# Backward of a gated linear-attention and feed-forward block on one core: grouped row-tile ends, a row vector spread through DRAM, other first loads

## The chip, the cores and the metric

The kernel runs on one core of a Trainium2 chip. The time is the device time of one execution in microseconds (us); lower is better. The kernel before took 638.77 us, the median of nine runs that lay between 637.89 and 639.11. The core has a matrix engine (TensorE, PE in the profile, with its weight loads as PEld), a vector engine (DVE), a scalar engine (ACT), a general engine (GpSimd, POOL) and a queue engine (SyncE, SP) that here issues transfers only. ACT issues transfers too. The engines run side by side, each in its own order, and wait for one another through semaphores.

## What is computed

The reference is a forward pass and its gradients. With x of 2048 tokens by 640, 32 heads of 20, and 1728 hidden columns:

```python
g = sigmoid((x * gate_w).sum(-1, keepdims=True))
q, k, v = heads of x @ wqkv
phi = lambda t: where(t > 0, t + 1, exp(t)) + 1e-6
kv = einsum("bhsd,bhse->bhde", phi(k), v)
z  = einsum("bhsd->bhd", phi(k))
o  = (phi(q) @ kv) / (phi(q) . z + 1e-6)
a  = o @ wo
b  = maximum(x @ w1, 0) @ w2
out = g * a + (1 - g) * b
```

The outputs are `out` and the gradients by x, wqkv, wo, w1, w2 and gate_w, all in bf16.

## The kernel before

The 2048 tokens are NT = 16 tiles of 128, in NG = 4 groups of G = 4. The 640 columns are KD = 5 blocks of 128. The 1728 hidden columns are KF = 14 blocks, of which the last has FT = 64 columns: its matmuls use half of the array's rows.

All long-lived data lie in one large buffer, the arena. A planner gives each named piece an offset and a life by nominal times (`ar.add(name, bytes, t0, t1)`, lines 113 to 189); pieces whose lives don't overlap share room. A change of one entry can therefore move other pieces. Small tiles come from pools: `tb` (8 buffers), `f32` (3), and PSUM tiles from `pp` (line 306), four buffers of two banks each. Code is written in program order, and the compiler's scheduler then orders each engine's instructions by priority and readiness; dependencies become waits. Only the opening stretch has its PE order fixed by hand (line 478).

The stages, in order, with their lines:

- k stage (399 to 511). First loads of x tiles 0 to 4 and the five blocks of wk, from SP and ACT. A few matmuls on a zeroed tile (`warm_up`) run until data are there. Tiles 0 to 4 of x are transposed on PE (`xt`), the rest by transposing transfers. Then k = x wk for each tile (`k_part`), with phi by `phi_chain`: exp on ACT, then two DVE operations (396, 397).
- Y stage (626 to 635). Y = phi(k)^T x, one 128-row block at a time. An extra column of ones in x gives z as a column of each block; it is copied to `zc_t`. To have z as a row on all partitions (`zb`), a diagonal matrix `zd` is made of each block of z, and a matmul of ones by `zd` (`zp`, 637 to 639) gives the row in PSUM; ACT copies it to `zb`. `q_den` (526) multiplies phi(q) by `zb` on POOL, and `q_post` (530) reduces the product on DVE.
- q, feed-forward forward and output (612 to 689). `h_half` makes half of a tile's hidden row, `out_chunk` the output. Here too `tail_pair` (579) ends two neighbouring tiles' sums together.
- dw2 and the gradient by q's factors (730 to 775), then X (801 to 808).
- The feed-forward backward (811 to 957), described below.
- dk (`dk_chunk`, 881) between halves of dw1 (`dw1_half`, 899), then dwk, dwq and dx (983 on).

In the feed-forward backward, `fb_a(i, half)` computes half of tile i's hidden gradient (PSUM tile `gp`), scales it on ACT, masks it on DVE, and after the second half starts the transposing transfer into a slot of the ring `hTb`. `fb_b(i)` multiplies the transposed tile by w1^T into a PSUM tile `dp`: thirteen blocks of two matmuls (512 and 128 columns, `mm_cols`, line 339), and the fourteenth block through `tail_pair`. That one runs two matmuls side by side, each on 64 rows: one ends tile i, the other starts tile i+1, for which a second `dp` is opened:

```python
nc.tensor.matmul(psA[:, b, 0:e - a], lhsT=lA[0:FT], rhs=rhs[0:FT, a:e], start=False, stop=last)
nc.tensor.matmul(psB[:, b, 0:e - a], lhsT=lB[FT:P], rhs=rhs[FT:P, a:e], start=True, stop=False)
```

So a tail pair comes once for every two tiles. ACT copies each finished `dp` out, and stores two tiles together to DRAM. The loop runs `fb_b` four tiles behind `fb_a`. Between them stand small products (`small_0` to `small_3`, PSUM tiles dwo, bd, qqp, dwv) and many loads. In iteration 14 of the loop the four groups of x^T for dk (`xSg`) and the first two loads of phi(k) are asked for.

Of the kernel before, what the change touches and what calls it, by code (L numbers as in the profile page):

```python
# [8 lines left out]
ALU = mybir.AluOpType  # L9
AX = mybir.AxisListType  # L10
FP32 = mybir.dt.float32
BF16 = mybir.dt.bfloat16
PSUM = bass.MemoryType.PSUM

P = 128
# [66 lines left out]
def kernel(  # L82
# [34 lines left out]
    def ring(name, elems, count, t0, t1):  # L117
        ar.add(name, elems * count * B2, t0, t1)
        rings[name] = [elems, count, 0]
# [13 lines left out]
    ar.add("w1", KD * F * B2, 8, T_H)  # L133
    ar.add("w2", KF * D * B2, 12, T_DW2 + 10)
    ar.add("pk", NT * D * B2, 0, T_FF)
    ar.add("zd", D * B2, 0, T_FF - 5)
    ar.add("YT0", KD * D * B2, T_Y, T_FF + 5)
    ar.add("dzs", D * B2, T_X, T_FB + 50)
    ar.add("warm", 512 * B2, 0, 10)
# [26 lines left out]
    ar.add("dKVT", KD * D * B2, T_FB + 40, T_FB + 65)  # L166
    ar.add("Q", KD * D * B2, T_FB + 58, T_DWK - 10)
    ar.add("N", KD * D * B2, T_DWK, T_END)
    ring("hTb", KF * P, 5, T_FB, T_DW1 + 5)
    ring("wst", D, 4, T_FB + 88, T_FB + 112)  # L170
    ar.add("dwoT", KD * D * B2, T_FB + 15, T_FB + 52)
    ar.add("dwo", KD * D * B2, T_FB + 45, T_FB + 80)
    ring("dxst", 2 * D, 2, T_FB + 5, T_DW1 + 5)
    ar.add("xN2", NT * D * B2, T_DW1 - 25, T_DX + 5)
    for g in range(NG):
        ar.add(f"xS{g}", G * P * KD * B2, T_DW1 - 25, T_DWK - 10)
        ar.add(f"dk{g}", G * D * B2, T_DW1 + 5 + 15 * g, T_DX)
        ar.add(f"dkT{g}", G * D * B2, T_DW1 + 5 + 15 * g, T_END)
    ring("pkr", 2 * D, 3, T_DW1 - 20, T_DWK)
# [15 lines left out]
    def aview(name, n_elems, **dims):  # L195
        o = ar.off(name) // 2
        v = arena[:, o:o + n_elems]
        if dims:
            (k, n), = dims.items()
            v = v.rearrange(f"p ({k} z) -> p {k} z", **{k: n})  # L200
        return v
# [7 lines left out]
    def mat(name):  # L209
        return aview(name, KD * D, k=KD)  # L210
# [15 lines left out]
    xSg = [aview(f"xS{g}", G * D, k=KD) for g in range(NG)]  # L226
    doTg = [aview(f"doT{g}", G * D, k=KD) for g in range(NG)]
    hsg = [aview(f"hs{g}", G * FPAD, i=G) for g in range(NG)]
    zd, YT0_s = aview("zd", D), mat("YT0")
    dzs = aview("dzs", D)  # L230
    wk_s, wq_s, wv_s, wo_s = aview("wk", KD * DQX, k=KD), mat("wq"), mat("wv"), mat("wo")
    w1_s = aview("w1", KD * F, k=KD)
# [30 lines left out]

    dram = ctx.enter_context(tc.tile_pool(name="dram", bufs=1, space=bass.MemoryType.DRAM))
    pk_d = dram.tile([S, D], BF16, name="pk_d")
    pqg_d = dram.tile([S, D], BF16, name="pqg_d")
    KVT_d = dram.tile([D, D], BF16, name="KVT_d")
    e_d = dram.tile([S, D], BF16, name="e_d")
# [14 lines left out]
                            pattern=[[-1, P]], channel_multiplier=1)  # L283
    gwb = cpool.tile([P, D], BF16, name="gwb")
    ones_sq = cpool.tile([P, P], BF16, name="ones_sq")
    zc_t = cpool.tile([P, KD], FP32, name="zc_t")
    MDw = cpool.tile([P, KD, BWID], BF16, name="MDw")
    zb = cpool.tile([P, D], BF16, name="zb")
    dzb = cpool.tile([P, D], BF16, name="dzb")
# [16 lines left out]
    def pp(name="pp"):  # L306
        return psp.tile([P, 2, 512], FP32, tag="PP", bufs=4, name=_nm(name))
# [4 lines left out]
    def csl(i):  # L312
        return slice(i * P, (i + 1) * P)

    def flat(ps_tile):
        return ps_tile.rearrange("p b c -> p (b c)")
# [16 lines left out]
    def load_N(dst, src):  # L333
        return nc.sync.dma_start(dst, src.rearrange("(i p) d -> p i d", p=P))
# [15 lines left out]
    def halves(ap):  # L350
        return ap.rearrange("p (b c) -> p b c", b=2)
# [47 lines left out]

    warm = aview("warm", 512)  # L400
    nc.vector.memset(warm, 0.0)
    def x_load(a, b):
        return load_N(xN[:, a:b, 0:D], x2[a * P:b * P, :])

    def wk_load(eng, k):
        eng.dma_start(wk_s[:, k, 0:D], A_wqkv[k * P:(k + 1) * P, D:2 * D])

    nc.scalar.dma_start(gst[:], gate_w.rearrange("(k p) -> k p", p=P))
    x_load(0, 1)
    wk_load(nc.scalar, 0)  # L410
    x_load(1, 2)
    wk_load(nc.scalar, 1)
    x_load(2, 3)
    wk_load(nc.scalar, 2)
    wk_load(nc.sync, 3)
    wk_load(nc.sync, 4)
    for i in range(3, NPE):
        x_load(i, i + 1)
# [40 lines left out]
    def warm_up(n, cols=512):  # L459
        for _ in range(n):  # L460
            nc.tensor.matmul(wp_[:, 0, 0:cols], lhsT=warm[:, 0:P], rhs=warm[:, 0:cols], start=True, stop=True)
# [16 lines left out]
    with tc.manual_schedule(engines={mybir.EngineType.PE}):  # L478
        warm_up(4)
        warm_up(1, 256)  # L480
        xt(0)
        tp = psp.tile([P, KD, P], BF16, tag="PP", bufs=4, name="gwtp")
        nc.tensor.transpose(tp[:, 0, 0:KD], gst[:], ident[0:KD, 0:KD])
        nc.vector.tensor_copy(wk_s[:, :, D:D + 1], tp[:, 0, 0:KD].unsqueeze(2))
        warm_up(3)
        k_part(0, [0])
        xt(1)
        xt(2)
        k_part(1, [0])
        k_part(0, [1])  # L490
        k_part(1, [1])
        k_part(2, [0, 1])
        k_part(0, [2])
        after(xT_ld[0], k_part(1, [2]), wait=True)
        k_part(2, [2])
        k_part(0, [4, 3])
        xt(3)
        k_part(1, [4, 3])
        xt(4)
        k_part(2, [4, 3])  # L500
        k_part(3, range(KD))
        k_part(4, range(KD))
# [123 lines left out]
    for m in range(KD):  # L626
        yp = pp("yp")
        for i in range(NT):
            mm_cols(yp, pkN[:, i, csl(m)], lambda a, e: xN[:, i, a:e], i == 0, i == NT - 1, spl=DSP1)
        yt = nc.scalar.copy(YT0_s[:, m, :], flat(yp)[:, 0:D])  # L630
        if m == 0:
            masks(yt)
        nc.vector.tensor_copy(zc_t[:, m:m + 1], flat(yp)[:, D:D + 1])
        nc.vector.tensor_scalar(zd[:, csl(m)], ident[:], zc_t[:, m:m + 1], None, ALU.mult)
        Y_ld = load_T(Y_s[:, :, csl(m)], YT0_s[:, m, :])
    h_half(0, 0)
    zp = pp("zp")
    mm_cols(zp, ones_sq[:], lambda a, e: zd[:, a:e], True, True)
    nc.scalar.copy(zb[:], flat(zp)[:, 0:D])
    q_den(0)  # L640
    h_half(0, 1)
    h_half(1, 0)
# [186 lines left out]
            load_T(dhTs[i], hs(i))  # L829

    def fb_b(i):
        pr, ii = i // 2, i % 2
        dT = dhTs.pop(i)
        if ii == 0:
            ops[i] = pp("dp")
        dp = ops.pop(i)
        for kf in range(KF - 1):
            mm_cols(dp, dT[:, kf, :], lambda a, e: w1T_s[:, kf, a:e], ii == 0 and kf == 0, ii == 1 and kf == KF - 2)
        if ii == 0:
            ops[i + 1] = pp("dp")  # L840
            tail_pair(dp, ops[i + 1], dT[:, KF - 1, :], dhTs[i + 1][:, KF - 1, :], w1T_s[:, KF - 1, :], True)
            dx_st[pr] = rnext("dxst").rearrange("p (i d) -> p i d", i=2)
        nc.scalar.copy(dx_st[pr][:, ii, :], flat(dp)[:, 0:D])
        if ii == 1:
            nc.scalar.dma_start(rows2(dxB_d, pr), dx_st.pop(pr))

# [19 lines left out]
    def small_3(ts):  # L866
        for t in ts:
            ps = pp("dwv")
            win_mms(ps, lambda j: YT_s[:, j, csl(t)], dKV_s)
            st = rnext("wst")  # L870
            nc.scalar.copy(halves(st), ps[:, :, 0:HD])
            nc.scalar.dma_start(out_2[csl(t), 2 * D:3 * D], st)


# [33 lines left out]
        nc.scalar.copy(st.rearrange("p (b c) -> p b c", b=2), wp[:, :, 0:NBW])  # L908
        nc.scalar.dma_start(out_4[csl(m), 2 * half * NBW:(2 * half + 2) * NBW], st)

    LAGB = 4
    smalls = {3: small_0, 7: small_2, 12: small_3}
    for i in range(NT + LAGB):
        if i < NT:
            fb_a(i, 0)
            if i in (0, 1):
                dz_add(NT - 2 + i)
            if i == 1:
                for m in range(KD):
                    load_T(XT_s[:, :, csl(m)], X_s[:, m, :])  # L920
            if i == 2:
                load_T(woT_s, A_wo)
            if i == 5:
                load_T(wvT_s, A_wqkv[:, 2 * D:3 * D])
            if i == 4:
                nc.sync.dma_start(dwoT_d.rearrange("(k p) d -> p k d", p=P), dwoT_s)
            if i == 6:
                nc.sync.dma_start(dKVT_d.rearrange("(k p) d -> p k d", p=P), dKVT_s)
                load_T(dwo_s, dwoT_d)
            if i == 8:  # L930
                nc.sync.dma_start(Q_d.rearrange("(k p) d -> p k d", p=P), Q_s)
                nc.sync.dma_start(out_3.rearrange("(i p) d -> p i d", p=P), dwo_s)
                nc.sync.dma_start(YT_s, YT_d.rearrange("(k p) d -> p k d", p=P))
            if i == 10:
                load_T(dKV_s, dKVT_d)
            if i in smalls:
                smalls[i](range(0, 2))
            if i % 2 == 0 or i == NT - 1:
                fb_a(i, 1)
        else:  # L940
            dw1_half(i - NT)
        if i >= LAGB:
            fb_b(i - LAGB)
        if i < NT - 1 and i % 2 == 1:
            fb_a(i, 1)
        if i == 5:
            small_1()
        if i in smalls:
            smalls[i](range(2, KD))
        if i == NT - 3:  # L950
            for g in range(NG):
                load_N(xN2[:, g * G:(g + 1) * G, :], x2[g * G * P:(g + 1) * G * P, :])
        if i == NT - 2:
            for g in range(NG):
                load_T(xSg[g], x2[g * G * P:(g + 1) * G * P, :])
            pk_load(0)
            pk_load(1)
    dk_chunk(0)
    dk_chunk(1)
    done = 2  # L960
    for n in range(LAGB, 2 * KD):
        dw1_half(n)
        while done < NT and done < n * 2 + 1:
            dk_chunk(done)
            done += 1
        if n == 8:
            for g in range(NG):
                load_N(dqN[:, g * G:(g + 1) * G, 0:D], dq_d[g * G * P:(g + 1) * G * P, :])
            nc.vector.tensor_copy(dqN[:, :, D:D + 1], dl_t[:].unsqueeze(2))
# [91 lines left out]
```

## Time and profile before

| What | Value |
|---|---|
| Median of nine runs | 638.77 us |
| The profiled execution's own time | 638.3 us |
| Its span, first to last instruction | 636.5 us |
| Granted TensorE clock, mean | 1.000 |
| k stage and before, up to 12 us: PE busy | 10.18 us |
| 319 to 470 us (feed-forward backward): PE busy, ACT busy, DVE busy | 149.87, 54.23, 45.98 us |
| DMA share in that stretch | 0.79 |

One execution was recorded by the hardware profiler. Its span is shorter than its own time by 1.8 us, which lie before the first and after the last instruction. Lines of the timeline read: start in us, length in us, engine, source line, operation, output from inputs, count; in brackets the idle time before it and what ended it. The ends of matmuls are modelled, so the time that a matmul really occupies PE is read from one start to the next. A few matmuls are missing from the records.

### The profile page before, as it was taken

The page shows a single profiled execution, that of the slowest core. Times are in us where ns is not written, and L with a number is a line of the kernel's source. Part 1 is how long each engine was busy: PE and PEld are TensorE (multiplying, and loading weights), DVE is VectorE, ACT ScalarE, POOL GpSimd, SP SyncE. Part 2 cuts the span into 40 slices and gives each one's busy share as a digit, 9 for nine tenths or more (in the row PEclk, how much of TensorE's full clock was granted, in tenths as well). Part 3 has the DMA queues.
Part 4 walks back from the last instruction along what each step waited for, and adds up shares of the span by engine and source line. Part 5 has one row for each costly group of instructions (what it writes and reads, how often), then busy time and mean ns, then how long its engine had stood idle before and what let it go on. Part 6 is the DMA issues. An engine that isn't in the chain of part 4 may idle for free.

```text
span 636.5 us, 10501 instructions
## 1 busy us (share of the span) xinstructions
PE 627.4 (99%) x4405; PEld 351.4 (55%) x4482; DVE 266.5 (42%) x520; ACT 150.0 (24%) x211; POOL 97.9 (15%) x95
## 2 busy tenths in 40 slices
PE   8999999999999999999999999999999999999998
PEld 4555555555555555555555555555555555555554
DVE  4832764454534146565994422220016320104442
ACT  4513321222221122222154433531110011110000
POOL 0050752454334022322001000000000000000000
PEclk9999999999999999999999999999999999999999
DMA  7999995544455693933989999972149569951111
GB/s 177 325 383 212 196 258 129 125 88 90 123 119 111 170 227 106 208 129 79 186 175 219 214 279 198 235 184 62 49 127 211 143 158 287 225 158 42 42 42 43
DMA packets 228473, 103.93 MB, mean 163 GB/s; under 512 B 185098, under 2 KB 227722, under 8 KB 228426
## 3 DMA queue, kind: packets, MB, share of 16 engines
q1 hardware_dynamic: 217344, 90.48, 61.9%
q10 hardware_dynamic: 11082, 12.79, 5.9%
q8 instruction: 35, 0.57, 0.4%
q14 instruction: 12, 0.10, 0.0%
HBM read 28.43 MB, written 28.84 MB: 90 GB/s over the span
## 4 chain that ended last, share of the span: by engine, by line
PE 97%; DVE 1%; issue 1%; ACT 1%; DVEq 0%; ACTq 0%
PE op L341 12%; PE dxp L341 10%; PE gp L818 9%; PE w1p L905 9%; PE w2p L341 9%; PE dp L341 9%; PE hp L565 9%; PE yp L341 3%; PE xp L341 3%; PE wkp L341 3%; PE rp L341 3%; PE dkp L341 3%; PE kp L341 3%; PE qp L341 3%; PE wqp L994 3%
## 5 line engine op out<-in xcount | busy, mean ns | idle before, releaser
L341 PEld LDWEIGHTS <-arena 128*128 128x128 bf16 x2978 | 230.8, 98 | 178.8 <-issue 0.8
L341 PE MATMUL op<-arena 128*128 128x128 bf16 (+1 forms) x567 | 79.1, 298 | 0.5
L565 PE MATMUL hp<-arena 128*128 128x432 bf16 x320 | 62.6, 346 | 0.0
L818 PE MATMUL gp<-arena 128*128 128x432 bf16 x320 | 61.2, 346 | 0.2
L341 PE MATMUL dxp<-arena 128*128 128x128 bf16 (+1 forms) x441 | 60.8, 297 | 0.5
L905 PE MATMUL w1p<-arena 128*128 128x432 bf16 x320 | 60.1, 346 | 0.0
L341 PE MATMUL w2p<-arena 128*128 128x128 bf16 (+1 forms) x408 | 58.5, 297 | 0.4
L341 PE MATMUL dp<-arena 128*128 128x512 bf16 (+1 forms) x400 | 57.9, 296 | 0.8
L905 PEld LDWEIGHTS <-arena 128*128 128x128 bf16 x320 | 30.8, 98 | 26.9 <-issue 0.5
L818 PEld LDWEIGHTS <-arena 128*128 128x128 bf16 x320 | 30.5, 98 | 27.0 <-issue 2.0
L565 PEld LDWEIGHTS <-arena 128*128 128x128 bf16 x320 | 29.9, 98 | 26.5 <-issue 1.8
L825 DVE TENSOR_TENSOR arena<-tb,tb 128x864 bf16<-128x864 bf16 x32 | 19.4, 606 | 53.6 <-ACT tb L822 53.0
L889 DVE TENSOR_TENSOR tb<-dkp,dzb 128x640 bf16<-128x640 f32 x16 | 13.1, 820 | 62.4 <-PE dkp L341 62.4
L822 ACT ACTIVATE tb<-gp,omg_t 128x864 bf16<-128x864 f32 x32 | 31.4, 981 | 30.4 <-PE gp L818 30.4
L604 DVE SCALAR_TENSOR_TENSOR tb<-op,arena 128x640 bf16<-128x640 f32 x16 | 13.1, 820 | 48.4 <-ACT arena L602 48.4
L528 POOL TENSOR_TENSOR f<-tb,zb 128x640 f32<-128x640 bf16 x16 | 23.4, 1463 | 61.2 <-DVE tb L397 50.4
L711 POOL TENSOR_TENSOR f<-zb,grd 128x640 f32<-128x640 bf16 x16 | 20.3, 1270 | 75.3 <-DVE grd L709 75.3
L602 ACT CAST arena<-op 128x640 bf16<-128x640 f32 x16 | 11.1, 692 | 81.8 <-PE op L341 47.2
L1018 DVE TENSOR_TENSOR arena<-dxp,f 128x640 bf16<-128x640 f32 x15 | 12.3, 823 | 36.8 <-PE dxp L341 36.8
L908 ACT CAST arena<-w1p 128x864 bf16<-128x864 f32 x10 | 8.8, 879 | 72.5 <-PE w1p L905 72.5
L542 POOL TENSOR_TENSOR arena<-tb,grd 128x640 bf16<-128x640 bf16 x16 | 20.3, 1270 | 29.1 <-DVE grd L536 22.3
L341 PE MATMUL rp<-arena 128*128 128x128 bf16 (+1 forms) x157 | 24.2, 297 | 0.2
(120 smaller groups left out, 608.6 us busy)
## 6 DMA issues: line engine op xcount, KB each, us to landing
out_dram<-arena ACTq DMA_DIRECT2D x28, 160.0 KB, 3.5
arena<-in_A_x_dram SPq DMA_DIRECT2D x6, 640.0 KB, 6.1
pk_d<-arena SPq DMA_DIRECT2D x4, 640.0 KB, 9.9
arena<-in_grad_out_dram SPq DMA_DIRECT2D x4, 640.0 KB, 4.8
e_d<-arena SPq DMA_DIRECT2D x8, 320.0 KB, 2.7
out_dram<-arena ACTq DMA_DIRECT2D x8, 320.0 KB, 2.3
arena<-e_d SPq DMA_DIRECT2D x8, 320.0 KB, 3.5
dq_d<-arena SPq DMA_DIRECT2D x8, 320.0 KB, 3.7
```

The source lines that it names most:

```text
L341: mm = nc.tensor.matmul(ps_tile[:, b, 0:e - a], lhsT=lhsT, rhs=rhs_fn(a, e), start=start, stop=stop, **kw)
L528: return nc.gpsimd.tensor_tensor(tzs[i][:], pqs[i][:], zb[:], ALU.mult)
L542: nc.gpsimd.tensor_tensor(heads(pg), heads(pq[:]), hb(grd[:]), ALU.mult)
L565: nc.tensor.matmul(hp[:, nb, 0:NBW], lhsT=xT(i, k), rhs=w1_s[:, k, blk * NBW:(blk + 1) * NBW], start=(k == 0), stop=(k == KD - 1))
L604: nc.vector.scalar_tensor_tensor(jk[:], flat(op)[:, 0:D], 1.0, doX(i)[:, 0:D], ALU.mult, ALU.mult, accum_out=T_t[:, i:i + 1])
L711: nc.gpsimd.tensor_tensor(heads(wz[:]), heads(zb[:]), hb(w32[:]), ALU.mult)
L818: nc.tensor.matmul(gp[:, nb, 0:NBW], lhsT=doTg[i // G][:, k, gsl(i)], rhs=w2T_s[:, k, blk * NBW:(blk + 1) * NBW], start=(k == 0), stop=(k ...
L822: nc.scalar.activation(gs[:], gp[:, :, 0:NBW], ACT.Copy, scale=omg_t[:, i:i + 1])
L825: nc.vector.tensor_tensor(hs(i)[:, rng], msk[:], gs[:].rearrange("p b c -> p (b c)"), ALU.mult)
L889: nc.vector.tensor_tensor(a_[:], flat(kp)[:, 0:D], dzb[:], ALU.add)
L905: nc.tensor.matmul(wp[:, nb, 0:NBW], lhsT=xN2[:, i, csl(m)], rhs=hs(i)[:, blk * NBW:(blk + 1) * NBW], start=(i == 0), stop=(i == NT - 1))
L994: nc.tensor.matmul(wp[:, 0, :], lhsT=lhsT, rhs=dqN[:, i, 0:512], start=(i == 0), stop=(i == NT - 1))
```

## The change

There are several edits.

1. Feed-forward backward. `fb_b(i)` now does only the thirteen full blocks. `fb_tails(i)` runs the tail pairs of tiles (i, i+1) and (i+2, i+3) in succession, opening two more `dp` tiles. `fb_out` holds the copy and the store. The loop goes by groups of four: tile i, then i+2, then both tail pairs, then i+1, then i+3, with the steps of the next group's `fb_a` (or the first `dw1_half`s) between. The ring `hTb` has six slots instead of five.
2. The x^T groups for dk and the first two loads of phi(k) are asked for at the first `dw1_half`, and their arena life starts there.
3. `zb`: `zd`, its five multiplies and the two `zp` matmuls are gone. `zc_t` becomes bf16 and is stored to DRAM (`z_d`), and `zb` is loaded from there with the row repeated on all partitions. Both transfers are on ACT's queue, and the second waits for the first.
4. First loads. SP issues x0, wk0, wk1, wk2, wk4; ACT issues gate_w, x1, x2, wk3. The second set of warm-up matmuls is one of 512 and one of 256 columns instead of three of 512. `xt(4)` stands directly behind `xt(3)`.
5. The copies of `dwv` go in turn to DVE and ACT.

```diff
-    ring("hTb", KF * P, 5, T_FB, T_DW1 + 5)
+    ring("hTb", KF * P, 6, T_FB, T_DW1 + 5)
...
-        ar.add(f"xS{g}", G * P * KD * B2, T_DW1 - 25, T_DWK - 10)
+        ar.add(f"xS{g}", G * P * KD * B2, T_DW1, T_DWK - 10)
...
     x_load(0, 1)
-    wk_load(nc.scalar, 0)
-    x_load(1, 2)
-    wk_load(nc.scalar, 1)
-    x_load(2, 3)
-    wk_load(nc.scalar, 2)
-    wk_load(nc.sync, 3)
+    wk_load(nc.sync, 0)
+    x_load(1, 2, nc.scalar)
+    wk_load(nc.sync, 1)
+    x_load(2, 3, nc.scalar)
+    wk_load(nc.sync, 2)
+    wk_load(nc.scalar, 3)
     wk_load(nc.sync, 4)
...
-        warm_up(3)
+        warm_up(1)
+        warm_up(1, 256)
...
         xt(3)
+        xt(4)
         k_part(1, [4, 3])
-        xt(4)
         k_part(2, [4, 3])
...
-        nc.vector.tensor_scalar(zd[:, csl(m)], ident[:], zc_t[:, m:m + 1], None, ALU.mult)
...
-    zp = pp("zp")
-    mm_cols(zp, ones_sq[:], lambda a, e: zd[:, a:e], True, True)
-    nc.scalar.copy(zb[:], flat(zp)[:, 0:D])
+    nc.scalar.dma_start(z_d.rearrange("(k p) -> p k", p=P), zc_t[:])
+    nc.scalar.dma_start(zb[:], z_d.rearrange("(o d) -> o d", o=1).to_broadcast([P, D]))
...
+    def fb_tails(i):
+        for t in (i, i + 2):
+            ops[t + 1] = pp("dp")
+            tail_pair(ops[t], ops[t + 1], dhTs[t][:, KF - 1, :], dhTs[t + 1][:, KF - 1, :], w1T_s[:, KF - 1, :], True)
+        fb_out(i)
+        fb_out(i + 2)
...
-            nc.scalar.copy(halves(st), ps[:, :, 0:HD])
+            copy_out(t + 1, halves(st), ps[:, :, 0:HD])
...
+    def step(i):
+        if i >= NT:
+            dw1_half(i - NT)
+            if i == NT:
+                for g in range(NG):
+                    load_T(xSg[g], x2[g * G * P:(g + 1) * G * P, :])
+                pk_load(0)
+                pk_load(1)
+            return
+        fb_a(i, 0)
...
+    for i in range(G):
+        step(i)
+    for i in range(0, NT, G):
+        step(i + G)
+        fb_b(i)
+        step(i + G + 1)
+        fb_b(i + 2)
+        fb_tails(i)
+        fb_b(i + 1)
+        if i == 0:
+            small_1()
+        step(i + G + 2)
+        fb_b(i + 3)
+        step(i + G + 3)
```

More of the change, by code (lines that the diff above doesn't have):

```diff
@@ L135 @@
     ar.add("pk", NT * D * B2, 0, T_FF)
-    ar.add("zd", D * B2, 0, T_FF - 5)
     ar.add("YT0", KD * D * B2, T_Y, T_FF + 5)
@@ L228 @@
     hsg = [aview(f"hs{g}", G * FPAD, i=G) for g in range(NG)]
-    zd, YT0_s = aview("zd", D), mat("YT0")
+    YT0_s = mat("YT0")
     dzs = aview("dzs", D)
@@ L265 @@
     pk_d = dram.tile([S, D], BF16, name="pk_d")
+    z_d = dram.tile([D], BF16, name="z_d")
     pqg_d = dram.tile([S, D], BF16, name="pqg_d")
@@ L285 @@
     ones_sq = cpool.tile([P, P], BF16, name="ones_sq")
-    zc_t = cpool.tile([P, KD], FP32, name="zc_t")
+    zc_t = cpool.tile([P, KD], BF16, name="zc_t")
     MDw = cpool.tile([P, KD, BWID], BF16, name="MDw")
@@ L401, with x_load @@
     nc.vector.memset(warm, 0.0)
-    def x_load(a, b):
-        return load_N(xN[:, a:b, 0:D], x2[a * P:b * P, :])
+    def x_load(a, b, eng=nc.sync):
+        return eng.dma_start(xN[:, a:b, 0:D], x2[a * P:b * P, :].rearrange("(i p) d -> p i d", p=P))
     def wk_load(eng, k):
@@ L831, in fb_b, with fb_out @@
     def fb_b(i):
+        if i % 2 == 0:
+            ops[i] = pp("dp")
+        dp, dT = ops[i], dhTs[i]
+        for kf in range(KF - 1):
+            mm_cols(dp, dT[:, kf, :], lambda a, e: w1T_s[:, kf, a:e], i % 2 == 0 and kf == 0,
+                    i % 2 == 1 and kf == KF - 2)
+        if i % 2 == 1:
+            fb_out(i)
[3 more added lines that the diff above has]
+            tail_pair(ops[t], ops[t + 1], dhTs[t][:, KF - 1, :], dhTs[t + 1][:, KF - 1, :], w1T_s[:, KF - 1, :], True)
+        fb_out(i)
+        fb_out(i + 2)
+    def fb_out(i):
         pr, ii = i // 2, i % 2
-        dT = dhTs.pop(i)
+        dhTs.pop(i)
         if ii == 0:
[L835 to L841, printed above, removed]
             dx_st[pr] = rnext("dxst").rearrange("p (i d) -> p i d", i=2)
-        nc.scalar.copy(dx_st[pr][:, ii, :], flat(dp)[:, 0:D])
+        nc.scalar.copy(dx_st[pr][:, ii, :], flat(ops.pop(i))[:, 0:D])
         if ii == 1:
@@ L909, in dw1_half @@
         nc.scalar.dma_start(out_4[csl(m), 2 * half * NBW:(2 * half + 2) * NBW], st)
-    LAGB = 4
     smalls = {3: small_0, 7: small_2, 12: small_3}
[L913 to L940, printed above, removed]
-            dw1_half(i - NT)
[L942 to L945, printed above, removed]
-        if i == 5:
-            small_1()
@@ new lines, in step @@
+    def step(i):
+        if i >= NT:
+            dw1_half(i - NT)
+            if i == NT:
[5 more added lines that the diff above has]
+        fb_a(i, 0)
+        if i in (0, 1):
+            dz_add(NT - 2 + i)
+        if i == 1:
+            for m in range(KD):
+                load_T(XT_s[:, :, csl(m)], X_s[:, m, :])
+        if i == 2:
+            load_T(woT_s, A_wo)
+        if i == 4:
+            nc.sync.dma_start(dwoT_d.rearrange("(k p) d -> p k d", p=P), dwoT_s)
+        if i == 5:
+            load_T(wvT_s, A_wqkv[:, 2 * D:3 * D])
+        if i == 6:
+            nc.sync.dma_start(dKVT_d.rearrange("(k p) d -> p k d", p=P), dKVT_s)
+            load_T(dwo_s, dwoT_d)
+        if i == 8:
+            nc.sync.dma_start(Q_d.rearrange("(k p) d -> p k d", p=P), Q_s)
+            nc.sync.dma_start(out_3.rearrange("(i p) d -> p i d", p=P), dwo_s)
+            nc.sync.dma_start(YT_s, YT_d.rearrange("(k p) d -> p k d", p=P))
+        if i == 10:
+            load_T(dKV_s, dKVT_d)
+        if i in smalls:
+            smalls[i](range(0, 2))
+        fb_a(i, 1)
@@ L952 @@
                 load_N(xN2[:, g * G:(g + 1) * G, :], x2[g * G * P:(g + 1) * G * P, :])
[L953 to L957, printed above, removed]
+    for i in range(G):
[12 more added lines that the diff above has]
+        step(i + G + 3)
     dk_chunk(0)
@@ L960 @@
     done = 2
-    for n in range(LAGB, 2 * KD):
+    for n in range(G, 2 * KD):
         dw1_half(n)
```

## The prediction

> **What bounds the kernel now.** I read the page's busy shares first, then the chain of waits as a whole, then the timeline at the three places that the edits touch.
>
> ```profile
> PE 627.4 (99%) x4405; PEld 351.4 (55%) x4482; DVE 266.5 (42%) x520; ACT 150.0 (24%) x211; POOL 97.9 (15%) x95
> ...
> PE 97%; DVE 1%; issue 1%; ACT 1%; DVEq 0%; ACTq 0%
> ```
>
> TensorE (PE) is the bound from end to end: 97% of the chain is PE, and where nothing interrupts it the stream is dense. The chain of waits shows pieces of 49 matmuls starting 6.79 us apart (574.35, 581.14, 587.93): one matmul missing from the records, so 25 pairs of 512 and 128 columns in 6.79 us, 0.272 us a pair. Only two things change the time: fewer PE columns, or fewer of PE's few stops. The stops are at row-tile changes (timeline, PE alone, then its weight loads):
>
> ```profile
> 339.14 3.69 PE L341 MATMUL dp<-arena 128*128 128x512 bf16 x25
> 342.76 0.39 PE L582 MATMUL dp<-arena 64*128 64x512 bf16 x1
> 342.77 0.39 PE L583 MATMUL dp<-arena 64*128 64x512 bf16 x1
> 342.99 0.22 PE L582 MATMUL dp<-arena 64*128 64x128 bf16 x1
> 342.99 0.22 PE L583 MATMUL dp<-arena 64*128 64x128 bf16 x1
> 343.14 1.09 PE L818 MATMUL gp<-arena 128*128 128x432 bf16 x5
> ...
> 342.76 0.09 PEld L582 LDWEIGHTS <-arena 64*128 64x128 bf16 x1 [0.26 <-issue]
> 343.14 0.84 PEld L818 LDWEIGHTS <-arena 128*128 128x128 bf16 x6 [0.27 <-issue]
> ```
>
> The two halves of a pair start together. The 26 matmuls ahead should take 13 x 0.272 = 3.53 us, so the pair was due at 342.67 and starts at 342.76: 0.09 lost going in. The pair's own stream is 0.27, so the next matmul was due at 343.03 and starts at 343.14: 0.11 lost going out. Together 0.20 us a change and back. The start and the place where zb is made (timeline):
>
> ```profile
> 3.95 1.46 PE L461 MATMUL warm<-arena 128*128 128x512 bf16 x3
> 5.20 0.52 PE L341 MATMUL kp<-arena 128*128 128x512 bf16 x2
> 9.73 0.49 DVE L347 COPY arena<-xtp 128x640 bf16<-128x640 bf16 x1 [2.94 <-PE xtp L449]
> 10.27 0.44 PE L449 MATMUL xtp<-ident,arena 128*128 128x128 bf16 x5
> 11.49 0.72 PE L341 MATMUL kp<-arena 128*128 128x512 bf16 x4 [0.24 <-DVE arena L397]
> ...
> 55.56 0.43 PE L341 MATMUL zp<-arena,ones_sq 128*128 128x512 bf16 x2
> 55.83 3.81 PE L565 MATMUL hp<-arena 128*128 128x432 bf16 x20
> 57.47 1.40 POOL L528 TENSOR_TENSOR f<-tb,zb 128x640 f32<-128x640 bf16 x1 [10.82 <-issue]
> 63.94 0.82 DVE L534 TENSOR_REDUCE grd<-f 128x32 f32<-128x640 f32 x1
> 67.30 0.47 PE L367 MATMUL mtp<-arena 128*128 128x140 bf16 x6 [0.26 <-DVE tb L397]
> ```
>
> [...] Here the three warm-ups of 512 columns take from 3.95 to 5.20, 0.42 us each, later ones of that width 0.22 (0.272 less a fifth), and the turn falls in the kp matmul at 5.20[...]; in the trace the 320 KB dxB stores from ACT land in 2.2 to 9.0 us, by what else is moving.
>
> **The change part by part.** The sum is made against the profiled execution: span 636.5, its own time 638.3, so 1.8 us lie around the span. The median of the nine runs is 638.77; a difference moves to it unchanged.
>
> (1) Row tiles. Per four token tiles the two tail pairs now stand in succession, so there are 4 changes instead of 8. 4 x 0.20 = 0.80 us less, if the second pair follows without a drain. The bounds: 0 (it drains too) to 0.9. Columns are the same. Cover needed: at the tails all four PSUM buffers are dp tiles. The two new ones take the buffers of the gp tiles of the step before; their evictions are 0.98 us each on ACT and have the 26 matmuls of fb_b(i+2), 3.53 us, to finish. After the tails two dp copies of 0.69 on ACT free buffers within the next 3.53 us. The dh^T transposes (4.1 us median to land) are read a whole group later than issued; the ring of 6 slots covers i to i+5. No stop is added there, and ACT, at 24%, has room.
>
> (2) zb. Gone are the two zp matmuls (55.56 to 55.83: 0.27 us of PE), the zb copy and five zd multiplies on DVE, off the path. Added on ACT's queue: a store of 640 two-byte elements, then a broadcast load of 160 KB that waits for it. zc is complete at about 54.8. Nothing in the trace gives the store's landing, so I bound it by 1.5 us (smallest landing of any store here) and 4 us; I take 2, so 57.0, just after the relu that ends at 56.74. Behind these two on ACT stand the relu of h(1,0), whose turn comes at 59.68, and the blockdiag copy at 61.08. A wait up to 59.4 costs nothing. The load, by rows of its size: 3.5 us median for ACT's 160 KB transfers, 6.0 for the gwb broadcast of the same shape, issued at 56.55. I take 3.5: zb at 60.5. POOL multiplies 1.40 us, done at 62.0. DVE reaches its reduce (63.94) after the masks, in the changed kernel 0.27 earlier, so zb may land until 63.67 - 1.40 - 0.06 = 62.2 at no cost. Behind that reduce DVE holds the L397 that PE waits for at 67.30, so every later us costs one us. Forecast: -0.27; range -0.3 to +2.5.
>
> (3) Start. Three warm-ups of 512 become one of 512 and one of 256, 0.64 us less at the half clock. The first kp then waits for DVE's xT copy (ends 4.76, weight load at 4.81) and starts near 4.92, but both its matmuls now run at half clock (0.43 + 0.11), ending at 5.46 instead of 5.56: 0.10 gained. wk0 is now SP's second load; the second one landed at 4.1 in the order of issue before (issue 1.25 plus 2.9), in time. xt(4) now stands directly behind xt(3). Both write one PSUM tile, and in the trace xt(4) starts at 10.27, when the DVE copy of xt(3) ends at 10.22. So PE stands: xt(3) 9.15, copy to 10.12, xt(4) 10.17 to 10.45, then eight kp matmuls, 4 x 0.272, to 11.54. Before, kp(3) starts at 11.49, after a stop for DVE L397. One stop is swapped for another: 0.0 net, bounds -0.4 (the 0.64 of warm-ups less what remains to wait) and +0.3 (x2, now on ACT, lands late).
>
> (4) The rest is moved under cover. The x^T transposes for dk leave the fb loop. Of the four, two stand ahead of the last dh^T in the built program's order on SP's queue; they took up to 5.9 us of issue each (352.35, 371.56), so it goes out about 10.4 us after the last gp, lands about 15, and is read at 5.84 + 3.53 + 5.84 + 3.53 = 18.7. dk itself starts some 38 us after the first of them. Three of the final base sums on DVE (2.48 us) now lie between two dk chunks where DVE idled 5.48. The dwv copies are split over ACT and DVE, but the wait for a buffer there (407.00 to 407.58, about 0.27) becomes one like that after dwo (0.29), since a gp eviction is what frees it. Net 0.0, bounds -0.3 and +0.3.
>
> Sum: -0.80 - 0.27 + 0 + 0 = -1.07; 638.3 becomes 637.2, and the median 638.77 becomes 637.7.
>
> **The rivals.** A: zb arrives late. Mechanism: POOL's first multiply waits, DVE's in-order queue stands at the reduce, mtp waits for L397. For it: ACT's 320 KB dxB stores took up to 9.0 us among transposes, and a transpose (59.34), an 800 KB store and a 640 KB load run at this very time. Against: 5.2 us of room between 57.0 and 62.2. It eats the gain of 1.07 from a landing at 63.3 on, and makes the kernel slower than before beyond that; at 9.0 us after issue, 66.0, it costs 3.8: 641.5. [...] C: the second pair drains as the first does, or the change is given back inside the group: -0.27 alone, 638.5. D: the shortened start comes through (warm-ups were all that held it): -0.5 more, 637.2.
>
> **How the numbers follow.** Forecast 0.45, A 0.20, B 0.10, C 0.09, D 0.16. 0.2% is 1.28 us, about what a measurement of this kernel can tell from no change, so faster means below 637.49 and slower above 640.05. The forecast's own range, 637.2 to 638.4, gives 0.14 faster and 0.31 same. D is 0.16 faster. A is 0.15 slower, 0.05 same. B is 0.02 slower, 0.08 same. C is 0.09 same. Sums: 0.30, 0.53, 0.17. The range reaches from D with a little of part (4), 636.8, to A with zb at 64.8, 640.3.
>
> **What would show it.** (1) is right if only four entries with 64-row weight loads waiting 0.26 remain among dp, and the second pair starts without such a wait. (2) is right if POOL's first L528-type multiply ends before DVE's first reduce would start, and mtp still waits about 0.26; a wait of that reduce on POOL is rival A. (3) is right if kp(3) starts at 11.5 +- 0.2 and the stop is before xt(4)[...]. A new wait of dp for a transpose, of gp for an ACT dp copy, or of dkp for an x^T load would make part (4) wrong.

## The result, and the profile after

The changed kernel takes 660.67 us (median of 9 runs, 656.29 to 663.22), the kernel before 638.77 beside it (29 runs): ratio 1.0338, 95% interval 1.0324 to 1.0352. It is slower by 22 us, where 1.1 us less was forecast. The profiled execution took 660.29 with a span of 658.6, so the 22.1 us by which the spans differ can be followed in one trace. The page of the changed kernel, the lines that answer to those of before (PEclk is the granted clock in tenths, for each fortieth of the span):

```profile
PE 631.5 (96%) x4403; PEld 353.3 (54%) x4479; DVE 264.5 (40%) x518; ACT 147.3 (22%) x207; POOL 98.0 (15%) x95
...
PEclk9999689999999999999998999999999999999999
...
PE 87%; DMA 5%; DVE 5%; issue 1%; ACT 1%; POOL 0%; ACTq 0%; DVEq 0%; POOLq 0%
```

PE is still the bound, but the chain now holds 5% of DMA and 5% of DVE, and the granted clock, at full speed throughout before, dips in two places (slices 5 and 6, and slice 22). I lined up the starts of the same groups of matmuls, named by the PSUM tile that they write, in both traces; the difference (after less before) changes only here:

| up to the start of | difference, us | what lies between |
|---|---|---|
| first qp (about 29 us) | -0.23 | the new start |
| first bd product | -0.50 | two zp matmuls gone |
| first mtp | +14.00 | a stop inside bd, then half clock |
| third qp | +18.56 | a stop ahead of mtp, then half clock |
| first dwo product (350) | +18.57 | nothing |
| first dp | +22.33 | a stop among the dwo products, then half clock |
| first w1p | +22.10 | three changes of row tiling saved, one stop at dwv |
| first dkp | +21.90 | the fourth change saved |
| end of the span | +22.1 | |

The chain of waits of the changed kernel at the first two stops (start, us, what):

```profile
54.62 17.01 DMA z_d<-zc_t
71.63 0.02 issue
71.66 8.26 DMA zb<-z_d
...
84.14 1.49 PE mtp L367 x12
```

The 1.2 KB store of z_d takes 17.0 us to land and the broadcast load of zb another 8.3. The timeline of PE at the same place, changed kernel:

```profile
59.07 0.76 PE L381 MATMUL bd<-arena 128*64 128x80 bf16 x31
...
71.84 0.82 PE L381 MATMUL bd<-arena 128*64 128x80 bf16 x19 [12.01 <-DMA arena<-arena]
...
72.59 3.78 PE L566 MATMUL hp<-arena 128*128 128x432 bf16 x10
```

Two things are to be seen. What bd waits for is not z_d: it is the last transpose of Y, on SP's queue, whose issue began 0.2 us ahead of z_d's and which landed with it, at 71.8 against 71.6. And the ten hp matmuls that follow take 3.78 us, as long as twenty took before: the trace's clock records have half rate (granted clock 0.50) from 63.04 to 76.70. So transfers that have nothing to do with the store land late with it; that the store holds them up is what store_only below shows.

The third stop, in the chain of the changed kernel around 316 to 356 us:

```profile
316.68 6.68 DMA f<-f
...
355.03 0.74 DVE arena L347
355.82 0.47 PE dwo L367 x6
```

f<-f shifts rows 64 to 127 of the gradient dw2's last tile to rows 0 to 63, inside SBUF. It landed after 3.5 us before and takes 6.7 now; POOL's addition waits for it, DVE's dz sums (L794, L796) wait for a buffer of that addition, and from there DVE runs late until the copy (L347) that frees a PSUM buffer for the third dwo product. No line of this was edited.

### The profile page after: what moved, and what is told of

Read it like the earlier page. It is cut to its first block, busy times and chain, and to the rows that moved or that the text cites. A ratio compares the mean times of both kernels' runs of the same rounds, so it can differ in the third digit from the quotient of the medians.

```text
span 658.6 us, 10495 instructions
## 1 busy us (share of the span) xinstructions
PE 631.5 (96%) x4403; PEld 353.3 (54%) x4479; DVE 264.5 (40%) x518; ACT 147.3 (22%) x207; POOL 98.0 (15%) x95
## 4 chain that ended last, share of the span: by engine, by line
PE 87%; DMA 5%; DVE 5%; issue 1%; ACT 1%; POOL 0%; ACTq 0%; DVEq 0%; POOLq 0%
PE op L341 12%; PE dxp L341 9%; PE w1p L916 9%; PE dp L341 9%; PE w2p L341 9%; PE hp L566 8%; PE gp L817 7%; PE yp L341 3%; PE wkp L341 3%; PE rp L341 3%; PE kp L341 3%; PE dkp L341 3%; PE qp L341 3%; DMA z_d<-zc_t 3%; PE wqp L1013 2%; DVE f L794 2%
## 5 line engine op out<-in xcount | busy, mean ns | idle before, releaser
L566 PE MATMUL hp<-arena 128*128 128x432 bf16 x320 | 64.9, 356 | 0.0
L341 PE MATMUL dp<-arena 128*128 128x128 bf16 (+1 forms) x402 | 58.3, 296 | 1.3 <-ACT tb L821 0.5
L341 PE MATMUL qp<-arena 128*128 128x128 bf16 (+1 forms) x151 | 24.0, 296 | 0.5
```

Source lines behind the costliest of these rows:

```text
L341: mm = nc.tensor.matmul(ps_tile[:, b, 0:e - a], lhsT=lhsT, rhs=rhs_fn(a, e), start=start, stop=stop, **kw)
L566: nc.tensor.matmul(hp[:, nb, 0:NBW], lhsT=xT(i, k), rhs=w1_s[:, k, blk * NBW:(blk + 1) * NBW], start=(k == 0), stop=(k == KD - 1))
```

## The experiments

Theory W says that the 640 two-byte writes of z_d hold the sixteen DMA engines for everybody; its rival Q says that the store is only one more transfer in a crowd and that the harm comes through ACT's queue, which waits for it. For the third stop, theory P says that the new list of buffers moved the addresses and with them the order of the loads; its rival G says that the new loop, which issues four gp steps ahead, makes DVE late. Medians are given with that of the kernel before on the same chip; in brackets stand their ratio and its 95% interval. In the code, "..." marks lines left out.

**zp_back**: the changed kernel with zb by the ones matmul (zd in a tile of its own, so that no address moves).

```diff
...
+        nc.vector.tensor_scalar(zd[:, csl(m)], ident[:], zc_t[:, m:m + 1], None, ALU.mult)
...
-    nc.scalar.dma_start(z_d.rearrange("(k p) -> p k", p=P), zc_t[:])
-    nc.scalar.dma_start(zb[:], z_d.rearrange("(o d) -> o d", o=1).to_broadcast([P, D]))
+    zp = pp("zp")
+    mm_cols(zp, ones_sq[:], lambda a, e: zd[:, a:e], True, True)
+    nc.scalar.copy(zb[:], flat(zp)[:, 0:D])
```

> The changed kernel, with zb made on chip again (diagonals, ones matmul, copy) and nothing else changed. Theory W (the 640 two-byte writes of z_d hold the DMA engines) and rival Q (z_d is only one more transfer in a crowd, and what hurts is the ACT queue behind it) agree here: the stops at bd and mtp go, which are +19.06 us of the +22.1 between the first bd and qp(2), and zp costs 0.27 again: span 658.6 - 19.1 + 0.3 = 639.8. If the stop of 2.2 us at the third dwo product (353.6) and its half-clock window (1.7) are only a consequence of the late start, they go too: 636.

Measured 641.13 beside 638.75 (ratio 1.0037, 1.0025 to 1.005). The stops at bd and mtp are gone; the one at dwo stays, 2.16 us from start to start (2.00 by the view, which models the ends), and its profiled execution has a mean granted clock of 1.000. So 19.5 of the 21.9 us by which the medians differ belong to z_d, and the stop at dwo is not its consequence. The profiled execution is the fastest of eight, 639.28; why the median lies 1.9 above it is open, since only one of the other seven shows less than the full clock.

**z_rows**: the changed kernel with the store in five rows of 256 bytes.

```diff
...
+    nc.tensor.transpose(zr[0:KD, 0, :], zc_t[:], ident[:])
+    nc.vector.tensor_copy(zr_t[:], zr[0:KD, 0, :])
-    nc.scalar.dma_start(z_d.rearrange("(k p) -> p k", p=P), zc_t[:])
+    nc.scalar.dma_start(z_d.rearrange("(k p) -> k p", p=P), zr_t[:])
```

> The changed kernel, with z turned on TensorE first, so that the store has 5 writes of 256 bytes in place of 640 of 2 bytes; the broadcast load and its place on ACT's queue stay. W: the store lands in 2 to 3 us, zb at about 62 to 64, no stop at bd, at most 2 us at mtp: span 639.5 to 642. Q: the store stands in the same crowd and lands after about 17 us as before: span 657 to 660.

Measured 641.05 beside 638.75 (1.004, 1.0025 to 1.0055), as W expects. The load of zb, which waits for the store, is issued 1.2 us after it, so the store had landed; the load itself takes 5.8 us. POOL's multiply by zb runs from 63.48 to 64.87, and beside it the last of ten mask products on DVE takes 1.37 us, where the nine others take 0.2 each. PE waits 0.60 us for that product, up to 64.98. The product in the chain of waits (start, us, what):

```profile
63.56 1.37 DVE arena L389
```

A second stop at mtp takes 0.26, as in the kernel before; zp_back has neither. Why the mask product is slow was not tested. Between the first and the third qp of the profiled executions z_rows is 1.0 us slower than zp_back and 0.8 slower than the kernel before: even with a store that lands within 1.2 us, this path looks worse there than the two matmuls it replaced. The medians, 641.05 and 641.13, don't show that difference.

**store_only**: the kernel before, with a store nobody waits for.

```diff
...
     h_half(0, 0)
+    nc.vector.tensor_copy(zc16[:], zc_t[:])
+    nc.scalar.dma_start(z_d.rearrange("(k p) -> p k", p=P), zc16[:])
     zp = pp("zp")
```

> The kernel before, with the 640 two-byte writes added at the same place and read by nobody; zb as before. W: the Y transposes, YT_d's store, gwb and the do load land 10 to 13 us later though nothing waits for z_d, PE stands at bd for about 12 us and the clock halves: 652 to 658. Q: nobody waits, so 638.8 within 0.5.

Measured 652.63 beside 638.75 (1.0226, 1.021 to 1.0241), with the same stop at bd, 12.3 us, though ACT's queue waits for nothing. Q falls. In the view of the DMA issues between 56 and 74 us (KB each, median us to landing), the kernel before and then store_only:

```profile
YT_d<-arena SPq DMA_DIRECT2D x1, 800.0 KB, 4.5
```

```profile
YT_d<-arena SPq DMA_DIRECT2D x1, 800.0 KB, 17.9
...
z_d<-zc ACTq DMA_DIRECT2D x1, 1.2 KB, 17.2
```

The store of Y^T, issued 0.7 us after z_d on the other queue, lands 1.3 us after it.

**store_spread** and **store_64**: store_only's 640 writes, each element 512 or 64 bytes from the next. Shown is the edit of store_64 against store_only; store_spread has 256 in place of 32.

```diff
-    z_d = dram.tile([D], BF16, name="z_d")
+    z_d = dram.tile([D, 32], BF16, name="z_d")
...
-    nc.scalar.dma_start(z_d.rearrange("(k p) -> p k", p=P), zc16[:])
+    nc.scalar.dma_start(z_d[:, 0].rearrange("(k p) -> p k", p=P), zc16[:])
```

> As store_only, but each two-byte element goes to a 512-byte block of its own. If the writes are slow because neighbours in one block wait for each other, the delay goes: 638 to 640. If every short write has its own price, it is as store_only: 652 to 658. Q: 638.8 within 0.5.

> As store_spread, but the two-byte elements stand 64 bytes apart. If neighbours wait for each other only within 64 bytes: 638.4, as store_spread. If within larger blocks of memory (512 bytes: 8 elements of a block in place of 256): a delay of a part of store_only's, 639 to 652.

Measured 638.42 beside 638.75 (0.9997, 0.9988 to 1.0005) and 638.44 beside 638.69 (0.9998, 0.9989 to 1.0006). The same view of store_64:

```profile
YT_d<-arena SPq DMA_DIRECT2D x1, 800.0 KB, 4.6
...
z_d<-zc ACTq DMA_DIRECT2D x1, 1.2 KB, 2.8
```

As many writes, as short, at the same point of the program: 2.8 us in place of 17.2. Neither the count of the writes nor their shortness costs here; it is that they go side by side into 1,280 bytes. Two bytes apart they add 13.9 us (652.63 beside 638.75), 64 bytes apart nothing that these intervals show (638.44 beside 638.69); no distance between the two was run.

**store_10b**: store_only with each partition's five elements side by side, `z_d.rearrange("(p k) -> p k", k=KD)`: 128 writes of 10 bytes.

> As store_only, but each partition writes its five elements side by side: 128 writes of 10 bytes, still several in each 64-byte block. If every write into a shared block has its price (13.9 us over 640 of them in store_only's time, some 17 us to land in the changed kernel, so 0.022 to 0.027 us each): 128 take about 3 us, most of it covered, 638.5 to 641. If the price hangs on the blocks alone (20 blocks in both): as store_only, 652.

Measured 638.81 beside 638.75 (1.0004, 0.9995 to 1.0012). The store lands in 3.2 us and Y^T's in 6.4. So the bytes touched, which are store_only's, don't set the price alone: fewer and longer writes into them cost little. The price is not shown to go in proportion: landing over writes is 0.025 us here and 0.027 in store_only, but the 2.8 us of a store that disturbs nobody are in both. Whether the distance from one write to the next counts or the narrow stretch of memory as a whole is open too.

**before_plan** and **before_plan_x**: the kernel before with the changed kernel's list of buffers. In the first the x^T loads for dk, at their old place, go into buffers that the new list still gives to others, and overwrite data that is still needed; only its time up to the first dp is used. The second issues these loads, and the first pk loads, after the last gp step.

```diff
-    ar.add("zd", D * B2, 0, T_FF - 5)
...
-    ring("hTb", KF * P, 5, T_FB, T_DW1 + 5)
+    ring("hTb", KF * P, 6, T_FB, T_DW1 + 5)
...
-        ar.add(f"xS{g}", G * P * KD * B2, T_DW1 - 25, T_DWK - 10)
+        ar.add(f"xS{g}", G * P * KD * B2, T_DW1, T_DWK - 10)
```

> The kernel before, line for line, but with the buffer list that the planner of the changed kernel was given (no zd in it, a ring of six for dh^T, x^T for dk later), so that the addresses are those of the changed kernel; zd lies outside. Theory P (addresses): the w1^T transposes go out ahead of the row shift of w2's tail, the shift lands 2 to 3 us later, DVE runs its dz sums that much later, and PE stops about 2.2 us ahead of the third dwo product: 640.4 to 643 (the upper end with a half-clock window). Rival G (the stop comes from the new loop, which issues four steps of gp ahead): 638.8 within 0.6.

> The kernel before with the changed kernel's buffer list, and with the x^T loads for dk and the first two pk loads issued after the loop's last gp step instead of two steps earlier, as that list needs. P: the row shift of w2's tail lands after 6 to 7 us in place of some 3.5, PE stops 2.2 us ahead of the third dwo product, and the whole takes 640.4 to 643. G: no such stop, 638.7 within 0.6.

The first shows the stop ahead of the third dwo product, 2.16 us (its whole time, 651.19, says nothing here). The second takes 641.19 beside 638.75 (1.0042, 1.0028 to 1.0055) with the old loop throughout. Its chain of waits, then its timeline:

```profile
298.44 6.45 DMA f<-f
```

```profile
337.38 0.53 PE L367 MATMUL dwo<-arena 128*128 128x140 bf16 x6 [2.00 <-DVE arena L347]
```

P, not G: the old loop has the stop. The two w1^T transposes on SP's queue, kernel before and then before_plan_x:

```profile
305.15 9.41 SPq L325 DMA_TRANSPOSE arena<-in_B_w_dram  x2
```

```profile
292.40 9.19 SPq L325 DMA_TRANSPOSE arena<-in_B_w_dram  x2
```

The shift is issued at 298.1 and 298.4: before the transposes in the one, among their packets in the other.

**zp_w1wait**: zp_back with the w1^T transposes waiting for POOL's addition.

```diff
-            nc.gpsimd.tensor_tensor(st[0:FT, :], w2e[0:FT, :], w2o[0:FT, :], ALU.add)
+            w2_add = nc.gpsimd.tensor_tensor(st[0:FT, :], w2e[0:FT, :], w2o[0:FT, :], ALU.add)
...
-        load_T(w1T_s[:, 0:KF - 1, ...], B_w1[...])
+        after(load_T(w1T_s[:, 0:KF - 1, ...], B_w1[...]), w2_add, wait=True)
```

> zp_back with one added wait: the two w1^T transposes go out only when POOL has added the shifted rows. P: the shift lands within 4 us, no stop ahead of the third dwo product; 641.1 less 2.2 and less what half-clock windows cost some runs: 638.2 to 639.2. G: the stop stays, 641 within 0.7.

Measured 638.10 beside 638.69 (0.9994, 0.9986 to 1.0002). POOL's addition starts at 301.11, 3.0 us after the shift is issued, and the stop ahead of the third dwo product is gone. One wait takes 3.0 us off zp_back, of which the stop explains 2.2.

**best1**: zp_w1wait with all dwv copies on ACT, as before the change (`nc.scalar.copy(halves(st), ...)` for `copy_out(t + 1, ...)`). **best2**: best1, with the first two dwv stores written after the gp step in the program text. **best2_oldstart**: best2 with the loads, warm-ups and xt(4) of the kernel before.

> zp_w1wait with all the dwv copies on ACT again, as before the change. P, and the 0.65 us stop ahead of dp after the last dwv product then shrinks to about 0.25: 637.8 to 638.8, so at most 0.4 us below zp_w1wait. If that stop comes from the issues of out_2's stores on ACT alone it stays: as zp_w1wait.

> best1 with the stores of the first two dwv tiles issued after the gp eviction that dp waits for, instead of ahead of it on ACT's queue. If ACT's 1.2 us of issues make the 0.5 us stop ahead of dp: it goes, 637.3 to 637.7, 0.4 to 0.5 below best1's 637.9. If the PSUM buffer comes late for another reason: 637.9 as best1.

> best2 with the first loads, the warm-ups and the place of xt(4) as in the kernel before. If the new start is worth what the recorded starts of both kinds say on average (29.46 less 29.21 us to the first qp): 0.25 us more than best2, with single starts scattered by half a us. If the scatter is all there is: as best2 within 0.15.

best1 takes 637.90 beside 638.69 (0.9989, 0.9982 to 0.9995), with the stop at dwv still 0.5. best2 says nothing on its question: the scheduler left the stores where they were on ACT's queue, ahead of the eviction, so it is a second best1: 638.43 beside 638.75 (1.0007, 0.9997 to 1.0018). best2_oldstart takes 638.78 (1.0006, 0.9998 to 1.0015), 0.35 more than best2, near the 0.25 expected but within what these two intervals leave open.

**before_grows**: the kernel before with its other store of 640 two-byte elements, the gate gradient, turned on TensorE and stored as five rows. **best3**: best1 with the same. **best4**: best3 with the two dwv stores forced behind the gp eviction.

```diff
-    nc.scalar.dma_start(out_6.rearrange("(k p) -> p k", p=P), gcol[:])
...
+            nc.tensor.transpose(gt[0:KD, 0, :], gcol[:], ident[:])
+            nc.scalar.copy(grow[:], gt[0:KD, 0, :])
+            nc.scalar.dma_start(out_6.rearrange("(k p) -> k p", p=P), grow[:])
```

> The kernel before, with the gate gradient (the other store of 640 two-byte elements, 569.8 us into the span, in both kernels) turned on TensorE during the second dx tile and stored as 5 rows of 256 bytes. If such a store holds the DMA engines wherever it stands, the 16 KB instruction load near 574, 2.3 to 3.5 us in every profile so far against 0.9 to 1.3 for the next ones, comes down to 0.9 to 1.5; the time 638.4 to 638.8. If that load is slow for another reason (dxB or out stores around it), it stays above 2.3.

> best1 with the gate gradient stored as rows as in before_grows. If the two-byte store makes the late instruction load and with it the stops of 0.5 to 1.4 us near 585 that three profiles of the changed loops show: 637.3 to 637.9 with a smaller spread than best1 and its twin best2 (637.4 to 641.6). If not: 637.9 to 638.4 with the same spread.

> best3 with the first two dwv stores really behind the gp eviction on ACT (in best2 the edit left ACT's order as it was). If the 1.2 us of issues cause the 0.5 us stop ahead of dp, it goes: 0.3 to 0.5 below best3. If not, as best3 within 0.15.

The 16 KB instruction load that follows it (near 574 us) takes 0.92 to 1.15 us in all three, where all fourteen other profiles, with the two-byte store, had 2.3 to 3.5 (best1 3.2, the kernel before 2.7): such a store holds other transfers there too. In time nothing comes of it: before_grows 638.85 beside 638.48 (1.0006, 0.9998 to 1.0015), best3 638.49 (1.0003, 0.9993 to 1.0013), no narrower than best1. That the PE stops of 0.35 to 0.89 us near 587 in three profiles (zp_w1wait, best2, best2_oldstart) come from the late load is therefore not shown. best4 takes 637.74 beside 638.48 (0.9990, 0.9982 to 0.9999). The timeline at the dwv stop, changed kernel first, then ACT in best4:

```profile
425.94 2.28 PE L341 MATMUL dp<-arena 128*128 128x512 bf16 x14 [0.52 <-ACT tb L821]
```

```profile
402.25 0.98 ACT L824 ACTIVATE tb<-gp,omg_t 128x864 bf16<-128x864 f32 x1 [0.30 <-PE gp L820]
```

In best4 the eviction starts when the gp product ends, instead of after 1.2 us of store issues as in best1 to best3, and dp no longer waits for it. best4 lies 0.75 below best3, more than the 0.5 expected, and 0.16 below best1. It is faster than the kernel before by 0.1%, at the edge of what its interval tells. best1's interval lies below 1 too, but its double best2 and best3 don't repeat that, so a gain of best1 is not shown.

## Why the prediction was wrong

**(1) Row tiles: right.** The groups of weight loads of 64 rows, with the idle time ahead of them and the part of it put down to "issue", kernel before and then changed kernel:

```profile
L582 PEld LDWEIGHTS <-arena 64*128 64x128 bf16 x32 | 1.8, 94 | 4.2 <-issue 4.2
```

```profile
L583 PEld LDWEIGHTS <-arena 64*128 64x128 bf16 x32 | 1.9, 94 | 3.6 <-issue 3.2
```

At 0.26 a change the 4.2 and 3.2 us of issue are 16 and 12 changes, four fewer. What the prediction calls a drain shows as this idle time of the weight loads. In the timeline of the changed kernel the second pair follows without it, and the way out is paid once:

```profile
372.56 0.38 PE L583 MATMUL dp<-arena 64*128 64x512 bf16 x1
...
372.92 3.38 PEld L341 LDWEIGHTS <-arena 128*128 128x128 bf16 x26 [0.26 <-issue]
```

Between the first dwo product and the first dkp best4 gains 0.83 us on store_spread, whose loop is the old one (some 0.2 of it can be that loop's own stop at dwv, so 0.6 to 0.8); 0.80 was forecast. Rival C is out.

**(2) zb through DRAM: wrong, and this is most of it.** The step that failed is "Nothing in the trace gives the store's landing, so I bound it by 1.5 us (smallest landing of any store here) and 4 us; I take 2". Ordinary stores gave the bounds, and this one isn't ordinary: 17.0. With 64 bytes between them, the same 640 writes land in 2.8; it is their lying side by side that the bounds didn't hold. And the trace of the kernel before did hold such a case: its gate gradient (gcol to out_6) is stored in the same form, a column of 640 two-byte elements. The view gives no landing for it, because only twelve of the sixteen semaphore signals that tell of a landing are recorded; but these twelve came 10.9 to 14.4 us after its issue at 569.79. With the row stores of before_grows, best3 and best4 the last signal came after 1.2. Put into the prediction's own sum in place of 2, 14.4 gives zb at 72.9 and, by an estimate, some 648 us in all.

The load was taken at 3.5 and has 8.3 here, 5.8 in z_rows. Rival A named the right place and the right chain at mtp: POOL waits for zb, DVE's reduce for POOL, and PE for DVE; only the operation that PE waits for is the copy L347 behind that reduce and not L397. It cost 4.6. The larger part, 14.5 at bd, was in no rival: all of them let the store delay only those who wait for it. For that stop the wait on ACT that I examined (relu, blockdiag copy) isn't needed: store_only has it without.

What I costed by stops alone was also short by the clock. After these stops PE ran at half rate for a while: 12.0 us of stop at bd cost 14.5, and the 2.2 at dwo 3.8. I had reckoned with the clock at the start only; here the three stretches at half rate last 13.65, 3.41 and 3.41 us, four, one and one times 3.41.

**(3) Start: right.** xt(4) starts at 9.91, after a stop for the copy of xt(3), and the kp matmuls from 10.40 put kp(3) at 11.49. Rival B was a start at half clock longer than before; what it would cost was an estimate of mine that no trace backed. The clock records have the full clock from 5.02, before from 5.36, so B is out. The first qp starts at 29.50 on average over nine profiles with the old start and at 29.35 over eight with the new one, each scattered by about half a us: 0.15 less, which at this scatter can't be told from the 0.0 forecast. The 0.5 of rival D doesn't show.

**(4) The rest: wrong.** "Net 0.0, bounds -0.3 and +0.3" came out as +3.8 at dwo, and as 0.5 at dwv where 0.29 was put. I went through what the edits of the loop move, and of the buffer list I only counted the slots of the ring. But with the new list the w1^T transposes stood ahead of the last dq_d store on SP's queue, as in before_plan_x, which has the stop with the old loop. That they moved because their addresses came free at another time is how I read it from the planner; which of the three edits of the list did it was not run. SP's order, which I had read for the x^T loads alone, was the thing to compare.

## What to carry to other kernels

Don't store a column of two-byte elements so that neighbours go out as single writes into one contiguous row: here that cost 13.9 us with no reader at all (store_only). Turn it first and store rows (the load behind them went out 1.2 us later in z_rows), or leave 64 bytes between the elements (2.8 us to land in store_64), and price such a store by all transfers in flight, not by its reader. Look for a transfer of the same form in the trace before you bound a new one by others. When the list of a planned arena changes, compare the order of every queue, above all of loads that the diff doesn't touch. A PE stop of 2 us or more can cost time beyond its length, 1.4 to 2.5 us at the three stops of the changed kernel; its length alone doesn't tell: after two stops of 2.00 us the profiled executions have a mean granted clock of 1.000 (zp_back) and 0.997 (before_plan_x).

## What the runs showed of the hardware

- Of 640 two-byte writes 64 bytes apart no transfer suffers by more than 0.8 us (2.8 to land, store_64); packed into 1,280 bytes they take 17.2 (store_only), and the transfers issued just before and after them on the other queue land with or after them. The packets don't tell: each of the 640 is recorded with 7 to 9 ns, while in the changed kernel the 159 packets of 1,280 bytes that start on the other queue between 58 and 66 us take 0.90 us on average, where 1,020 took 0.069 before. These runs show that neighbours cost, not by what mechanism; shortness alone, 64 bytes apart, cost no time (638.44 beside 638.69).
- In the trace of the changed kernel the granted clock goes to 0.50 and back at 63.04, 76.70, 83.52, 86.94, 356.59 and 360.00 us, which are whole numbers of 3.413 us apart: 4, 6, 7, 86 and 87 times that after the first.
- PE's busy share was counted in stretches of that length on that grid, with the modelled ends, in the same trace. At full rate, the stretches with 6% (from 59.63), 18% (from 80.11) and 42% (from 353.18) were followed by half rate; the least that was followed by full rate is 63% (from 653.55). At half rate, 0% (from 63.04 and 66.45) and 42% (from 69.87) were followed by half rate, 82% (from 83.52) and 100% (from 73.28 and 356.59) by full. What happens between 42% and 63%, or between 42% and 82%, this trace doesn't show.
